# Dilated and plain sliding-window attention with a gated FFN: residue-order attention blocks, v turned on chip, and a list scheduler that sets every engine's order

## Chip, cores and metric

The kernel runs on one core of a Trainium2 chip. The metric is the device time of one execution in microseconds. Before the change it is 392.39 us, the median of three runs (391.03 to 394.54); the profiled execution spans 389.0 us from its first to its last instruction. TensorE (PE in the profile, with PEld for its weight loads), VectorE (DVE), ScalarE (ACT), GpSimd (POOL) and SyncE (SP) each run their own queue in order, and DMA transfers are issued from the queues of POOL (loads) and SP (stores).

## The reference

Shapes: 8 batches, 8 heads, 576 positions, head size 64; the FFN has 512 inputs, 1024 hidden, 512 outputs. Everything comes and goes in float32.

```python
scores = (1/sqrt(64)) * q @ k.T
rel = pos[:, None] - pos[None, :]
mask_plain = (rel >= 0) & (rel < 32)                       # heads 0 to 3
mask_dil   = (rel >= 0) & (rel < 128) & (rel % 4 == 0)     # heads 4 to 7
attn = softmax(where(mask, scores, -1e9))
x = (attn @ v) as [8*576 tokens, 8*64]
out = ((x @ w1) * (x @ w2)) @ w3 @ w_out
```

A query of the first four heads sees at most 32 preceding positions (its own among them); a query of the last four sees every fourth of the 128 preceding ones, which are positions of its own residue modulo 4.

## The kernel before

**The FFN.** `w3 @ w_out` is multiplied once into `wf` (`fuse_t`, L383, turns a slice of w3 on TensorE; `fuse_m`, L392, multiplies). The 4608 tokens go in 9 tiles of 512. For each tile `ffn1` (L341) does, for 8 slices of the hidden size, four matmuls of 512 columns with w1 into one PSUM bank, ACT's copy of them to SBUF (L360), four with w2 into another bank, and VectorE's product of the two (L361). `ffn2` (L363) multiplies the gated tile with `wf`, 8 matmuls for each 128 tokens; ACT copies the result and SP stores it. All three use the PSUM tag `f`, with three banks.

**Attention.** A batch has four steps (class `Step`, L191): head group u = 0 (plain) or 1 (dilated), in two halves each. `transposes` (L180) turns q and k of one group with VectorE, so that partitions hold 32 of the 64 head dimensions of four heads; a position then takes two bf16 values, 4 bytes. It is called from within `scores` when a group begins, that is, it enters VectorE's queue just before the matmuls that need it. `scores(hp)` (L196) does two of the four heads: plain heads in blocks of 96 queries and 128 keys, at contiguous positions; dilated heads in blocks of 72 queries of one residue, read with a step of four positions from the same tile:

```python
lhsT=kt[prt, k0 : k0 + st * (P - 1) + 1 : st, c],
rhs=qt[prt, q0 : q0 + st * (nq - 1) + 1 : st, c],      # st is 1 or 4
```

ACT takes the exponential (L225), VectorE multiplies by a 0/1 mask (L230). `values` (L245) multiplies by v, which has a column of ones, so that the sums come along (L258 plain, L274 dilated); `norm` (L234) divides on VectorE; `xpose` (L283) turns the result on TensorE (L290, L302) and copies it into `XT`, the FFN's input, in token order: plain heads by VectorE (L296), dilated ones by ACT, with a step of four tokens (L309).

**v.** It is loaded twice over in ready form: `vp` (L102) with 32 rows of overlap between blocks for plain heads, and `vd` (L120), eight DMAs a batch, for dilated heads.

**Order.** Each engine's order is the order of the program. Loads are issued at the start (L408 to L421): q, k and v of batch 0, then w1 and w2, then q, k, v of batch 1, w_out and w3. Batch 0's attention is written in full before any FFN work. Afterwards `point()` (L434), called inside the FFN's loops, puts in pieces of the later batches' attention by a table of marks (`np.interp` over `xs`, `ys`); when a batch's pieces are done, the loads of the next but one are issued on POOL. PSUM: scores two banks, values two, transposes one, FFN three.

Of the kernel before, what the change touches and what calls it, by code (L numbers as in the profile page):

```python
# [10 lines left out]
P = 128  # L11
# [8 lines left out]
S = 576  # L20
D = 64
ROWS = 18
HALF = 288
PADK = 32
PITCH = 80
ETW = 4 * HALF + 64
TB = 512


@with_exitstack  # L30
def kernel(
# [22 lines left out]
    ctx.enter_context(tc.manual_schedule())  # L54

    const = ctx.enter_context(tc.tile_pool(name="const", bufs=1))
    qk_pool = ctx.enter_context(tc.tile_pool(name="qk", bufs=2))
    tr_pool = ctx.enter_context(tc.tile_pool(name="tr", bufs=2))
# [3 lines left out]
    ps_o = ctx.enter_context(tc.tile_pool(name="pso", bufs=1, space=bass.MemoryType.PSUM))  # L62
    ps_x = ctx.enter_context(tc.tile_pool(name="psx", bufs=1, space=bass.MemoryType.PSUM))
    ps_f = ctx.enter_context(tc.tile_pool(name="psf", bufs=3, space=bass.MemoryType.PSUM))
# [7 lines left out]
    mask_pl = const.tile([P, 2, 3, 96], BF16, name="mask_pl")  # L72
    mask_di = const.tile([P, 2, 2, 72], BF16, name="mask_di")
    NV = 2
    vps = [const.tile([P, 24, PITCH], BF16, name=f"vp{i}") for i in range(NV)]
    vds = [const.tile([P, 4, 2, 4, PITCH], BF16, name=f"vd{i}") for i in range(NV)]
    NET = 3
    ets = [const.tile([P, ETW], BF16, name=f"et{i}") for i in range(NET)]
    NKT = 2
    kts = [const.tile([P, PADK + S, 2], BF16, name=f"kt{i}") for i in range(NKT)]  # L80
    qts = [const.tile([P, S, 2], BF16, name=f"qt{i}") for i in range(NKT)]
# [4 lines left out]
    def load_qk(b, us=(0, 1), both=True):  # L86
        for nm, src in (("qn", q), ("kn", k)):
            if (nm, b) not in qk:
                qk[(nm, b)] = qk_pool.tile([P, 2, ROWS * D], BF16, tag=nm, name=nm)
            t = qk[(nm, b)]  # L90
            flat = src[b].rearrange("(u h) s d -> u (h s d)", u=2)
            if both:
                nc.gpsimd.dma_start(
                    out=t, in_=flat.rearrange("u (p x) -> p u x", p=P)
                )
            else:
                for u in us:
                    nc.gpsimd.dma_start(
                        out=t[:, u, :], in_=flat[u].rearrange("(p x) -> p x", p=P)
                    )  # L100

    def load_vp(b):  # L102
        vp = vps[b % NV]
        base = v[b, 0, 0, 0:1]
        off = base.offset

        def src(p0, n, j0, nj):
            return bass.AP(
                tensor=base.tensor,
                offset=off + (96 * j0 - 32 + p0) * D,  # L110
                ap=[[D, n], [96 * D, nj], [1, D]],
            )

        if b == 0:
            nc.gpsimd.dma_start(out=vp[32:P, 0:1, 0:D], in_=src(32, 96, 0, 1))
            nc.gpsimd.dma_start(out=vp[:, 1:24, 0:D], in_=src(0, P, 1, 23))
        else:
            nc.gpsimd.dma_start(out=vp[:, :, 0:D], in_=src(0, P, 0, 24))

    def load_vd(b):  # L120
        vd = vds[b % NV]
        for h in range(4):
            for w in range(2):
                nc.gpsimd.dma_start(  # L124
                    out=vd[:, h, w, :, 0:D],
                    in_=v[b, 4 + h, 64 * w : 64 * w + 512, :].rearrange(
                        "(p r) d -> p r d", r=4
                    ),
                )

    def load_w12(c):
        for dst, src in ((w1_sb, moe_w1), (w2_sb, moe_w2)):
            nc.gpsimd.dma_start(
                out=dst[:, :, 256 * c : 256 * (c + 1)],
                in_=src[:, 256 * c : 256 * (c + 1)].rearrange("(a p) f -> p a f", p=P),
            )

    def load_wo():
        nc.gpsimd.dma_start(out=wo_sb, in_=moe_w_out.rearrange("(a p) f -> p a f", p=P))

    w3t = {}

    def load_w3(ft):
        w3t[ft] = w3_pool.tile([P, d_ff], BF16, tag="w3", name="w3n")
        nc.gpsimd.dma_start(out=w3t[ft], in_=moe_w3[ft * P : (ft + 1) * P, :])


    def build_constants():
        make_identity(nc, ident)
        for t in ets:  # L150
            nc.gpsimd.memset(t[:, 4 * HALF : ETW], 0.0)
        for t in kts:
            nc.gpsimd.memset(t[:, 0:PADK, :], 0.0)
        for t in vps:
            nc.gpsimd.memset(t[:, :, D : D + 1], 1.0)
        for t in vds:
            nc.gpsimd.memset(t[:, :, :, :, D : D + 1], 1.0)
        nc.gpsimd.memset(vps[0][0:32, 0:1, 0:D], 0.0)
        nc.gpsimd.memset(mask_pl, 1.0)
        nc.gpsimd.affine_select(  # L160
            out=mask_pl, in_=mask_pl, compare_op=AL.is_ge, fill=0.0,
            base=32, pattern=[[0, 2], [0, 3], [1, 96]], channel_multiplier=-1,
        )
        nc.gpsimd.affine_select(
            out=mask_pl, in_=mask_pl, compare_op=AL.is_ge, fill=0.0,
            base=-1, pattern=[[0, 2], [0, 3], [-1, 96]], channel_multiplier=1,
        )
        nc.gpsimd.memset(mask_pl[0:32, 0, 0, :], 0.0)
        nc.gpsimd.memset(mask_di, 1.0)
        nc.gpsimd.affine_select(  # L170
            out=mask_di, in_=mask_di, compare_op=AL.is_ge, fill=0.0,
            base=0, pattern=[[0, 2], [56, 2], [1, 72]], channel_multiplier=-1,
        )
        nc.gpsimd.affine_select(
            out=mask_di, in_=mask_di, compare_op=AL.is_ge, fill=0.0,
            base=31, pattern=[[0, 2], [-56, 2], [-1, 72]], channel_multiplier=1,
        )


    def transposes(b, u):  # L180
        for nm, dst, pad in (("qn", qts[u], 0), ("kn", kts[u], PADK)):
            t = qk[(nm, b)]
            nc.vector.transpose(  # L183
                out=dst[:, pad : pad + S, :]
                .rearrange("p s c -> p (s c)")
                .bitcast(U32)
                .rearrange("p (j a) -> p a j", a=ROWS),
                in_=t[:, u, :].bitcast(U32).rearrange("p (a i) -> p a i", a=ROWS),
            )

    class Step:  # L191
        def __init__(self, n, b, u, hf):
            self.n, self.b, self.u, self.hf = n, b, u, hf
            self.et = ets[n % NET]

        def scores(self, hp):  # L196
            u, hf = self.u, self.hf
            if hf == 0 and hp == 0:
                transposes(self.b, u)
            qt, kt = qts[u], kts[u]  # L200
            sp = ps_s.tile([P, 2, TB], F32, tag="s", name="sp")
            if u == 0:
                blocks = [
                    (96 * (3 * hf + m), 96 * (3 * hf + m), 96, 96 * m, 1) for m in range(3)
                ]
            else:
                blocks = []
                for bl in range(4):
                    r, w = 2 * hf + bl // 2, bl % 2
                    blocks.append((PADK + 64 * w + r, 288 * w + r, 72, 72 * bl, 4))  # L210
            for k0, q0, nq, c0, st in blocks:
                for c in range(2):
                    for g in range(2):
                        prt = slice(32 * (2 * hp + g), 32 * (2 * hp + g) + 32)
                        nc.tensor.matmul(  # L215
                            out=sp[:, g, c0 : c0 + nq],
                            lhsT=kt[prt, k0 : k0 + st * (P - 1) + 1 : st, c],
                            rhs=qt[prt, q0 : q0 + st * (nq - 1) + 1 : st, c],
                            start=(c == 0),
                            stop=(c == 1),  # L220
                        )
            ev = self.et[:, 2 * hp * HALF : 2 * (hp + 1) * HALF].rearrange(
                "p (g x) -> p g x", g=2
            )
            nc.scalar.activation(out=ev, in_=sp[:, :, 0:HALF], func=ACT.Exp, scale=scale)  # L225
            if u == 0:
                mk = mask_pl[:, hf, :, :].rearrange("p m x -> p (m x)")
            else:
                mk = mask_di.rearrange("p r w x -> p (r w x)")
            nc.vector.tensor_tensor(  # L230
                out=ev, in0=ev, in1=mk.unsqueeze(1).to_broadcast([P, 2, HALF]), op=AL.mult
            )

        def norm(self, o, nq, nj, xo):  # L234
            rcp = wk_pool.tile([P, 2, 6], F32, tag="rcp", name="rcp")
            ov = o[0:nq, :, 0 : nj * (D + 1)].rearrange("p h (j e) -> p h j e", e=D + 1)
# [126 lines left out]
    def ffn2(t, tb, point):  # L363
        point()
        y = ps_f.tile([P, d_model], F32, tag="f", name="y")
        for f in range(KFF):
            if f == KFF // 2:
                point()
# [131 lines left out]
```

The softmax here doesn't subtract the row's maximum and nothing guards it: scores larger than these inputs give would overflow.

## Time and profile before

| | before |
|---|---|
| time, median of 3 | 392.39 us |
| span of the profiled execution | 389.0 us |
| mean granted TensorE clock | 0.918 |
| matmuls of `ab` (ffn1), `y` (ffn2), `wf` in the trace | 548, 275, 61; mean 406, 403, 422 ns |
| scores: dilated, plain | 512 matmuls, mean 314 ns; 384, mean 234 ns |
| POOL: issues of `vd` | 64, 743 ns each |
| HBM read, written | 44.03 MB, 9.44 MB |

How to read it: a row of a group gives the line, the engine, the operands with partitions x elements, the count, then busy time and the mean of one, then how long the engine had been idle before such instructions and what ended that. A matmul's duration contains its way through the array; several are in flight, so the distance between starts, not the duration, is what one costs. The trace lacks a few matmul records (548 of 576 `ab`). The 40 digits of a slice row are tenths of busy time in slices of 9.7 us. In a timeline, "x12" merges twelve instructions that follow each other, and the number after the start is the time from the first's start to the last's end. The PEclk row has no record ahead of 46 us and shows 9 there.

### The profile page before, as it was taken

How to read it: one execution, taken by the hardware profiler on the slowest of the kernel's cores; microseconds unless marked ns; L12 is line 12 of the kernel's file. 1: busy time of each engine (PE TensorE's matmuls, PEld its weight loads, DVE VectorE, ACT ScalarE, POOL GpSimd, SP SyncE). 2: the span in 40 equal slices, each digit the busy share in tenths (PEclk: the TensorE clock that was granted, in tenths of full speed). 3: DMA queues.
4: the chain of work that ended last, by engine and by line, in shares of the span. 5: the costliest groups of instructions: out<-in, count | busy, mean ns of one | idle time of the engine just before them, and what ended most of it. 6: DMA issues, size and time to landing. Idle time of an engine off the chain costs nothing. (4 is left out here: it accounts for less than half of the span.)

```text
span 389.0 us, 6039 instructions
## 1 busy us (share of the span) xinstructions
PE 314.3 (81%) x2516; PEld 166.6 (43%) x2560; DVE 171.7 (44%) x288; ACT 135.9 (35%) x213; POOL 87.4 (22%) x131
## 2 busy tenths in 40 slices
PE   0382768887887989987987979697969798899995
PEld 0261335343553545443543445254534354444442
DVE  2553456455344453566335644455354644222220
ACT  1222314441443433434342523252325234433332
POOL 8884544632000521015200620060000000000000
PEclk9999989796997998999896989798988899999998
DMA  3999999996600579009920977072000000111103
GB/s 62 150 167 199 152 207 198 157 119 124 41 2 0 35 128 185 33 29 82 176 41 27 83 122 96 27 70 40 28 2 27 29 27 31 51 56 54 53 32 136
DMA packets 74492, 31.86 MB, mean 82 GB/s; under 512 B 59616, under 2 KB 64736, under 8 KB 74464
## 3 DMA queue, kind: packets, MB, share of 16 engines
q0 software_dynamic: 69280, 22.02, 52.5%
q1 hardware_dynamic: 5184, 9.44, 6.5%
q8 instruction: 20, 0.33, 0.3%
q14 instruction: 8, 0.07, 0.0%
HBM read 44.03 MB, written 9.44 MB: 137 GB/s over the span
## 5 line engine op out<-in xcount | busy, mean ns | idle before, releaser
L350 PE MATMUL ab<-XT,w_sb 128*128 128x512 bf16 x548 | 151.2, 406 | 9.1 <-ACT XT L309 6.4
L215 PE MATMUL sp<-qt,kt 32*128 32x72 bf16 (+1 forms) x896 | 58.3, 279 | 46.9 <-DVE kt L183 44.0
L350 PEld LDWEIGHTS <-w_sb 128*128 128x128 bf16 x576 | 53.2, 103 | 63.0 <-issue 17.8
L225 ACT ACTIVATE et<-sp 128x576 bf16<-128x576 f32 x64 | 41.8, 653 | 100.9 <-PE sp L215 100.9
L124 POOL DMA_DIRECT2D vd<-in_v_dram x64 | 47.2, 743 | 130.3 <-PE o L274 109.2
L215 PEld LDWEIGHTS <-kt 32*128 32x128 bf16 x896 | 43.5, 128 | 74.4 <-DVE kt L183 43.6
L369 PE MATMUL y<-wf_sb,gt 128*128 128x512 bf16 x275 | 74.2, 403 | 1.1 <-issue 0.8
L361 DVE TENSOR_TENSOR gt<-ab,asb 128x512 bf16<-128x512 f32 x72 | 49.6, 689 | 57.6 <-PE ab L350 56.6
L360 ACT CAST asb<-ab 128x512 bf16<-128x512 f32 x72 | 42.1, 585 | 72.7 <-PE ab L350 61.5
L369 PEld LDWEIGHTS <-gt 128*128 128x128 bf16 x288 | 26.7, 101 | 36.0 <-issue 10.5
L230 DVE TENSOR_TENSOR et<-et,mask_di 128x576 bf16<-128x576 bf16 x32 | 14.7, 458 | 57.5 <-ACT et L225 57.5
L377 ACT COPY osb<-y 128x512 f32<-128x512 f32 x36 | 21.1, 585 | 50.1 <-PE y L369 47.0
L238 DVE TENSOR_TENSOR xo<-o,rcp 72x512 bf16<-72x512 f32 (+1 forms) x48 | 37.2, 775 | 1.7
L230 DVE TENSOR_TENSOR et<-et,mask_pl 128x576 bf16<-128x576 bf16 x32 | 14.7, 458 | 40.4 <-ACT et L225 39.9
L309 ACT COPY XT<-x 128x288 bf16<-128x288 bf16 x32 | 23.1, 852 | 14.5 <-PE x L302 14.5
L183 DVE STREAM_TRANSPOSE qt<-qn 128x576 uint32<-128x576 uint32 x16 | 20.0, 1249 | 8.2 <-DMA qn<-in_q_dram 8.2
L237 DVE RECIPROCAL rcp<-o 72x8 f32<-72x8 f32 (+1 forms) x48 | 10.1, 210 | 27.3 <-PE o L258 14.3
L183 DVE STREAM_TRANSPOSE kt<-kn 128x576 uint32<-128x576 uint32 x16 | 19.8, 1239 | 1.9 <-DMA kn<-in_k_dram 1.9
L398 PE MATMUL wf<-wo_sb,w3T 128*128 128x512 bf16 x61 | 17.5, 422 | 0.4 <-issue 0.3
L274 PEld LDWEIGHTS <-et 128*128 128x128 bf16 x256 | 13.6, 108 | 9.6 <-issue 2.4
L274 PE MATMUL o<-vd,et 128*128 128x65 bf16 x256 | 15.1, 208 | 1.3 <-DVE xo L238 1.2
L302 PE MATMUL x<-ident,xo 72*128 72x72 bf16 x128 | 9.7, 206 | 7.0 <-DVE xo L238 5.7
(40 smaller groups left out, 122.8 us busy)
## 6 DMA issues: line engine op xcount, KB each, us to landing
out_dram<-osb SPq DMA_DIRECT2D x36, 256.0 KB, 2.0
vd<-in_v_dram POOLq DMA_DIRECT2D x64, 64.0 KB, 3.9
qn<-in_q_dram POOLq DMA_DIRECT2D x7, 576.0 KB, 6.3
kn<-in_k_dram POOLq DMA_DIRECT2D x7, 576.0 KB, 9.2
vp<-in_v_dram POOLq DMA_DIRECT2D x7, 384.0 KB, 7.9
w_sb<-in_moe_w_dram POOLq DMA_DIRECT2D x8, 256.0 KB, 7.2
w3n<-in_moe_w_dram POOLq DMA_DIRECT2D x8, 256.0 KB, 11.5
wo_sb<-in_moe_w_out_dram POOLq DMA_DIRECT2D x1, 1024.0 KB, 9.2
```

The lines of the kernel that those rows point to most:

```text
L124: nc.gpsimd.dma_start(out=vd[:, h, w, :, 0:D], in_=v[b, 4 + h, 64 * w : 64 * w + 512, :].rearrange("(p r) d -> p r d", r=4),)
L183: nc.vector.transpose(out=dst[:, pad : pad + S, :] .rearrange("p s c -> p (s c)") .bitcast(U32) .rearrange("p (j a) -> p a j", a=ROWS), in ...
L215: nc.tensor.matmul(out=sp[:, g, c0 : c0 + nq], lhsT=kt[prt, k0 : k0 + st * (P - 1) + 1 : st, c], rhs=qt[prt, q0 : q0 + st * (nq - 1) + 1 : ...
L225: nc.scalar.activation(out=ev, in_=sp[:, :, 0:HALF], func=ACT.Exp, scale=scale)
L230: nc.vector.tensor_tensor(out=ev, in0=ev, in1=mk.unsqueeze(1).to_broadcast([P, 2, HALF]), op=AL.mult)
L238: nc.vector.tensor_tensor(out=xo[0:nq, :, 0:nj, :], in0=ov[:, :, :, 0:D], in1=rcp[0:nq, :, 0:nj].unsqueeze(3).to_broadcast([nq, 2, nj, D]) ...
L274: nc.tensor.matmul(out=o[:, hp, j * (D + 1) : (j + 1) * (D + 1)], lhsT=self.et[:, c0 : c0 + P], rhs=vd[:, h, w, 2 * self.hf + r, 0 : D + 1 ...
L309: nc.scalar.copy(out=dst[:, 2 * self.hf + r, :, :], in_=xv[:, r, :, :])
L350: nc.tensor.matmul(out=ps, lhsT=w_sb[:, c, f * P : (f + 1) * P], rhs=XT[:, c, t0 : t0 + TB], start=(c == 0), stop=(c == DCH - 1),)
L360: nc.scalar.copy(out=a_sb, in_=ps)
L361: nc.vector.tensor_tensor(out=gts[t][:, f, :], in0=pss[1], in1=a_sb, op=AL.mult)
L369: nc.tensor.matmul(out=y, lhsT=gts[t][:, f, tb * P : (tb + 1) * P], rhs=wf_sb[:, f, :], start=(f == 0), stop=(f == KFF - 1),)
```

## The change

The kernel is rewritten around the same FFN. It does this:

- **Residue order.** q is turned so that positions lie by residue modulo 4 (144 positions each), and for dilated heads k too. Both groups then use blocks of 96 queries against 128 keys at contiguous places, and one step does all four heads, on four row groups of the array, into four PSUM banks. Where a block of 96 crosses from one residue to the next, the mask cuts it. `XT` holds tokens in residue order, and the stores put each row back at its place in the output, four rows apart.
- **Bias in batches 0 and 1.** There, a matmul with the identity puts a large negative bias into PSUM ahead of the scores, and the multiplication by the mask falls away. Later batches multiply by the mask, as before.
- **v turned on chip in batches 0 and 1.** v is loaded like q and k in long rows, turned by VectorE, then on TensorE (`v_back`), and copied to its place by ACT or VectorE (`v_keep`). Later batches load v without overlap (one DMA for plain heads, eight for dilated ones), and VectorE copies the 32 rows of overlap (`halo_v`).
- **Weights** come in halves; constants other than the masks move from POOL to VectorE; 24 matmuls on a tile of zeros run at the start.
- **PSUM**: scores four banks in one buffer; four banks, as places that the scheduler gives out, for FFN, values and transposes.
- **A list scheduler.** Every piece of work is a `Task` with an engine, an assumed duration, the tasks that it needs, and a priority. `Plan.run` simulates the five engines with these numbers and gives an order; the instructions are then written out in it. Attention has priority on TensorE, and the scores of later batches are held back until the FFN has come so far (`paced`, LEAD). Loads come in a fixed order: q and k of batch 0, its v, w1 and w2, w_out, w3, then batch 1.

Its purpose is to shorten the work of attention, to let the FFN begin before batch 1 is loaded, and to keep TensorE from waiting. The diff, cut to its core:

```diff
+class Plan:
+    def run(self):
...
+                for e in engines:
+                    if free[e] > now:
+                        continue
...
+                    for r, t in waiting[e]:
+                        if r > now or (t.slot and not open_):
+                            continue
+                        if best is None or t.prio < best[1].prio:
+                            best = (r, t)
...
+    ets = [const.tile([P, 4 * VC + 32], BF16, name=f"et{i}") for i in range(4)]
+    kts = [const.tile([P, 2, PADK + S, 2], BF16, name=f"kt{i}") for i in range(2)]
+    qts = [const.tile([P, 2, S, 2], BF16, name=f"qt{i}") for i in range(2)]
...
+    def halo_v(b):
+        vp = vps[b % 2]
+        nc.vector.tensor_copy(out=vp[0:32, :, 1:6, 0:D], in_=vp[96:128, :, 0:5, 0:D])
...
+    def v_back(b, u, half):
+        x = bank([P, 3, 2, P], BF16, "vx")
+        for mm in range(3):
+            n0 = QB * (3 * half + mm)
+            for c in range(2):
+                nc.tensor.transpose(
+                    out=x[:, mm, c, :], in_=vts[0][:, u, n0 : n0 + P, c], identity=ident
...
+            self.sp = ps_s.tile([P, 4, TB], F32, tag="s", name="sp")
+            if biased:
+                for g in range(4):
+                    nc.tensor.matmul(
+                        out=self.sp[:, g, 0:VC],
+                        lhsT=ident,
+                        rhs=bias[:, self.kind(), :, :],
+                        start=True,
+                        stop=False,
+                    )
+            for mm in range(3):
+                m = 3 * hf + mm
+                for c in range(2):
+                    for g in range(4):
+                        prt = slice(32 * g, 32 * g + 32)
...
+                        nc.tensor.matmul(
+                            out=self.sp[:, g, QB * mm : QB * mm + QB],
+                            lhsT=kt[prt, u, QB * m : QB * m + P, c],
+                            rhs=qq,
...
+            row = b * S + 4 * (x % RUN) + x // RUN
+            nc.sync.dma_start(
+                out=out[row : row + 4 * (n - 1) + 1 : 4, :], in_=o_sb[at - c0 : at - c0 + n, :]
+            )
...
+    for u in range(2):
+        loads_rows("qn", 0, (u,))
+        loads_rows("kn", 0, (u,))
+    loads_rows("vn", 0)
...
+    lw12 = [loads_w12(0), loads_w12(1)]
...
+                s = add("S" + n, "PE", 480, T[u], st.scores, b - 99, after=[prev["s"]])
+                e = add("E" + n, "ACT", 1150, [s], st.exps, 10 * b + 1, lat=100, after=[prev["e"][i]])
+                m = add("M" + n, "DVE", 680, [e, mk], st.masks, 10 * b + 2, lat=80)
...
+        a = add(f"A{t}.{f}", "PE", 864, need + wl + free, lambda: up(t, f, w1_sb, "a"), seq, slot=True)
...
+    for b, i, t in paced:
+        pair = int(9 * (b - LEAD) + 2.25 * i)
+        if pair > 0:
+            t.after.append(pairs[pair])
+            t.deps.append(pairs[pair])
+
+    order, _ = plan.run()
+    for t in order:
+        plan.now = t
+        t.fn()
```

## The prediction

> **What bounds the kernel now.** I read the page's busy table and 40 slices first, then TensorE's waits between 46 and 332 us, then the timeline around the longest of them.
>
> ```profile
> span 389.0 us, 6039 instructions
> PE 314.3 (81%) x2516; PEld 166.6 (43%) x2560; DVE 171.7 (44%) x288; ACT 135.9 (35%) x213; POOL 87.4 (22%) x131
> PE   0382768887887989987987979697969798899995
> PEclk9999989796997998999896989798988899999998
> ```
>
> TensorE is the bound, but 81% flatters it, since a busy matmul need not be at its peak. The true floor: FFN matmuls of 512 columns follow each other every 216 ns in the chain of waits at the end (16 of `ab` in 3.45 us). There are 576 of `ab`, 288 of `y` and 64 of `wf`: 928 x 0.216 = 200 us. The rest of 389 us is attention, idle time and a slow clock. TensorE's waits from 46 to 332 us:
>
> ```profile
> PE sp L215 <- DVE kt L183: 26.4, 12, 3.1
> PE ab L350 <- ACT XT L309: 5.5, 7, 0.9
> PE x L302 <- DVE xo L238: 3.8, 6, 1.3
> ```
>
> One wait dominates: scores wait for the two transposes that `scores` itself puts at the end of VectorE's queue at each change of head group. All other waits of TensorE in this stretch add to 15 us. One of the twelve, in the timeline:
>
> ```profile
> 204.07 0.69 DVE L361 TENSOR_TENSOR gt<-ab,asb 128x512 bf16<-128x512 f32 x1 [2.30 <-PE ab L350]
> 204.68 1.25 DVE L183 STREAM_TRANSPOSE qt<-qn 128x576 uint32<-128x576 uint32 x1
> 205.76 1.24 DVE L183 STREAM_TRANSPOSE kt<-kn 128x576 uint32<-128x576 uint32 x1
> ...
> 207.06 0.66 PE L215 MATMUL sp<-qt,kt 32*128 32x96 bf16 x12 [2.17 <-DVE kt L183]
> ```
>
> These 12 matmuls take 0.66 us; a group of the same form takes 0.43 at 166.71 (below). The stall has also cost the clock. The clock record after 46 us holds twelve stretches at half speed, 3.4 or 6.8 us each, 61 us in all; windows of 2 us show an empty or half-empty PE just ahead of nearly all of them. Half of 61 is 31 us of lost work. The 9s of the first PEclk slices deceive: at 42 us `ab` matmuls still come every 0.43 us, so everything before 46 us ran cold.
>
> Last, what attention costs a warm TensorE:
>
> ```profile
> 158.53 1.28 PE L215 MATMUL sp<-qt,kt 32*128 32x72 bf16 x16
> ...
> 159.74 0.60 PE L369 MATMUL y<-wf_sb,gt 128*128 128x512 bf16 x2
> ```
> ```profile
> 166.70 0.29 PEld L215 LDWEIGHTS <-kt 32*128 32x128 bf16 x12 [2.46 <-DVE kt L183]
> 166.71 0.43 PE L215 MATMUL sp<-qt,kt 32*128 32x96 bf16 x12 [0.92 <-DVE kt L183]
> 167.07 0.55 PEld L350 LDWEIGHTS <-w_sb 128*128 128x128 bf16 x4
> 167.07 1.04 PE L350 MATMUL ab<-XT,w_sb 128*128 128x512 bf16 x4
> ```
>
> Read from the start of a group to the start of the next: dilated scores hold PE 1.21 us for 16 (76 ns each), plain ones 0.36 for 12 (30 ns). Value matmuls take 31 ns each (8 in 0.25 at 168.81), transposes of 96 columns some 42. A batch is thus 4 x 1.21 + 4 x 0.36 scores, 56 x 0.031 values and about 1 of transposes: 9 us, 72 for eight. Check from 46 to 332 us: FFN and w3 151, attention 62, slow clock 31, idle 41: 285 of 286.
>
> **What the skill says.** SBUF — State Buffer, "Door 1: The DMA port swizzle", has SBUF read in 16-byte lines, with a penalty where each access goes to a new one. Dilated q and k are read at every fourth position of 4 bytes: 16 bytes, a line each; 76 ns against 30 agrees. TensorE: Matmul & The Clock Gate, "Part 1: The HAM clock gate", says that an idle window (about 3.4 us) halves PE's clock and a busy one restores it; the stretches of 3.4 and 6.8 us agree, though gaps of 2 to 3 us already set them off here. The same page, "Back-to-back issue gap", gives N/2.4 + 2.5 ns per warm matmul: 216 at 512, as measured. VectorE: DVE Perf Modes, "The perf-mode tier table", gives an SBUF bf16 copy of 2048 elements as 693 ns; no row here shows one.
>
> **The change, part by part.**
>
> *Residue order and 96-query blocks.* Both head groups now have 96 queries per block, on four row groups at once, from contiguous 4-byte steps: 24 matmuls per step, four steps per batch. The strided 76 ns goes. Per step: at 30 ns each 0.72 us; if the four row groups leave only the weight loads, 0.29/12 x 24 = 0.58. I take 0.65; with values 12 x 0.031 = 0.37 and six transposes 0.25, a step is 1.27 and a batch 5.1, against 9. That saves 3.9 us a batch, 27 for batches 1 to 7, all on the bounding engine. The kept copies get cheaper too: the stride-4 XT copies of ACT (852 ns for 288) become runs of 24 or more, at 160 + 0.83 ns an element by ACT's rows of 512 (585) and 1024 (1012): 0.40.
>
> *Bias instead of mask, v turned on chip, both in batches 0 and 1.* Batch 1 gets 16 bias matmuls of 288 columns, 122 ns each by the formula: 2.0 us; and 24 transposes of v at 56 ns: 1.3. It loses four mask multiplies on VectorE. Batch 0's lie in the head.
>
> *VectorE's order.* Transposes are now put ahead by the scheduler, with two buffers of whole batches. I cost the wait at nothing where a batch's loads are early: VectorE has the room to hide them. Its load per batch of 9 FFN pairs, with slopes from rows (f32 from PSUM 155 + 1.04 ns an element; bf16 158 + 0.52): gates 9 x 0.69 = 6.2, masks 4 x 0.76 = 3.0, reciprocals 8 x 0.2 = 1.6, norms of 384 elements 8 x 0.55 = 4.4, kept copies 4 x 0.31 = 1.2, transposes about 5.2 (the split ones pay a fixed cost twice), halo copy of 2560 elements 0.8 by the skill's price, 2.7 at one element a cycle. Sum 22.5 to 24.3. TensorE needs, per batch, 9 x 1.73 + 4.5 x 1.73 + 5.1 = 28.4. VectorE is 79 to 86% busy: not the bound, but tight. ACT: 9 + 4.5 copies x 0.585, four exps of 1152 elements at 1.13, four copies: 14 of 28.
>
> *PSUM.* Scores take four banks in one buffer; FFN, values and transposes share four. Behind an A matmul group waiting for a bank stands everything on PE. A bank is held 1.7 us by a group of `ab` (0.86 fill, 0.69 evacuation), so two groups in flight leave two banks for attention. I keep the 15 us of other waits in 286 us, 5%, as the rate of such stalls: 0.05 x 243 = 12 us.
>
> *The head.* Before, the first `ab` starts at 42 us. Batch 1's q and k are issued behind ten v loads, w1 and w2, and PE's queue puts their scores first: it sits idle 6.3 us until 39.6. Now tile 0's FFN follows batch 0 alone. POOL makes five q, k, v issues and the masks (eleven instructions of 0.2 to 1 us) by 10.5 us. Then four steps, each held by its exp: warm 0.65 + 0.5 bias + 0.15 + 1.13 = 2.4, cold (12 scores took 0.60 at 11.3 us) 3.6; then values, norms, transposes and copies of the last step, 3.2. Batch 0 ends between 23 and 28 us; I take 26. w1 and w2 are there: 3.9 MB at some 190 GB/s (the fourth and seventh of the DMA slices show 199 and 198), from 3.3 us, is 24 us. Until batch 1 is there (8.8 MB, 50 us, plus 10 to 12 for its chain) PE has tile 0 (13.8), w3's fusing (17.4), `y` of tile 0 (6.9) and batch 1's own 8.4: 46 us of work, so the gap is filled. The 24 warm-up matmuls lie beside loading. I add 2 us for a first cold window at 26 us.
>
> *Stores.* Rows four apart, about 67 DMAs of 2 KB rows instead of 36. SP's queue does nothing else and the queue's share is 6.5%: nothing.
>
> *Loads.* v drops from 14.7 to 9.4 MB read; batches 2 to 7 issue nine v DMAs each on POOL, as now, and POOL is 22% busy: nothing.
>
> **Sum.** TensorE work from 26 us: 200.4 + 64 x 0.056 for w3 + 6 x 5.1 + 8.4 = 243. Span 26 + 2 + 243 + 12 + 4 (last matmul to the end, as now) = 287; the time exceeds the span by 3.4 us now. Forecast 290 us.
> From above: 392 - 16 (head) - 26 (transpose wait) - 31 (clock) - 27 (scores) + 3 (bias, v) = 295, before any gain on the other idle waits. The two ways agree; I take 290.
>
> **Rivals.**
> A, the clock keeps halving: VectorE, four fifths busy and strictly in order, delays evacuations, PE pauses 2 us here and there, and half the clock stretches stay. For: gaps of 2 us were enough before. Against: the transposes, the one long wait, move ahead. If the clock is at half for 21% of the stretch as now (61 of 286), PE loses 0.11 x 243 = 27 us: 317.
> B, the head gains nothing: batch 0 takes until 42 us as the first `ab` does now, as DMA or the longer mask building holds it. For: POOL and DMA are busy nearly the whole head. Against: fewer bytes come first. 290 + 16 = 306.
> C, even better: no stalls, scores at 0.58: 290 - 12 - 2 = 276.
> D, slower than before: the fixed orders don't fit the chip, each engine waits in its own order for another's, and the clock, once half, stays there as it did until 46 us. Attention's stretch holds about 190 us of PE work; at half speed for 60% of it, +114: 404. Against: slots and in-order waits existed before, with only 15 us of them.
>
> **How the numbers follow.** Forecast (280 to 302) 0.60; A 0.18; B 0.10; C 0.07; D 0.05. The likeliest is 290. Range: down to 272 (no stalls, 23 us head, scores 0.58), up to 322 (A, with the halo copy at its slow price). What is left out is D and the far ends of A and C. Faster by over 1%: all but D, and a little of A gone further: 0.94; same 0.01; slower 0.05.
>
> **What would show it.** Right: no wait of scores for `kt` beyond 2 us after 60 us; at most two or three half-clock stretches past 70 us; dilated and plain scores both under 0.75 us for 24; first `ab` at 24 to 30 us; VectorE near 65% busy and PE over 90% from 60 us on. Wrong: `ab` or `y` waiting for banks freed by VectorE for over 20 us in sum, half clock in the middle, or PE idle between 45 and 70 us for batch 1.

## The result, and the profile after

The changed kernel takes 277.59 us (median of four runs, 276.21 to 278.35) against 391.71 us before in the same series; the ratio is 0.709, with a 95% interval of 0.704 to 0.714. The forecast was 290 us. The kernel before takes 382 to 394 us from one execution to the next, and its profiled one is among the slower, so savings on it are counted below from its faster executions, with medians of 382.6, 383.1 and 382.9 us in the three later series. Counted so, the changed kernel saves 105 us and not 114. The changed kernel itself ran in the first series only, so differences of 1 to 2 us from it say little.

The page of the changed kernel, in the lines that answer to those shown of before:

```profile
span 274.5 us, 5945 instructions
PE 258.3 (94%) x2440; PEld 132.8 (48%) x2440; DVE 168.6 (61%) x342; ACT 124.7 (45%) x207; POOL 65.7 (24%) x105
PE   8577997899889989999999999999999999999993
DVE  3674435999999989999799555566654232242220
PEclk9989999999999999999999999999999999999999
```

TensorE's row is 9 almost throughout, and its clock row is now honest: the clock record begins at 5.6 us, with one stretch at half speed at 12.5 us (3.4 us) and none until the kernel is over. The 7 at 41 us and the 8 behind it are a hole that run 11 is about. VectorE shows mostly 9 from the eighth to the twenty-second slice (48 to 151 us), more than I had reckoned.

TensorE's waits from 24 us to the end, longest first:

```profile
PE x L412 <- DVE xo L401: 1.3, 3, 0.7
PE wf L506 <- ACT w3T L501: 1.2, 1, 1.2
PE x L494 <- DVE wf_sb L516: 1.1, 2, 0.8
PE sp L344 <- DVE qt L289: 0.8, 1, 0.8
PE ab L442 <- ACT asb L453: 0.7, 1, 0.7
```

Scores wait for turned q or k once, 0.8 us; all waits of this view add to 5.7 us. The timeline shows why, and what a step of attention costs:

```profile
147.24 0.44 PE L344 MATMUL sp<-qt,kt 32*128 32x96 bf16 x24
147.35 0.31 DVE L431 COPY XT<-x 128x288 bf16<-128x288 bf16 x1
147.61 1.04 PE L442 MATMUL ab<-XT,w_sb 128*128 128x512 bf16 x4
147.69 0.40 ACT L429 COPY XT<-x 128x288 bf16<-128x288 bf16 x1
147.73 1.41 DVE L289 STREAM_TRANSPOSE kt<-kn 128x320 uint32<-128x320 uint32 x2
```

The transposes run while TensorE is in the FFN and nothing waits for them. The 24 score matmuls of a step take 0.37 us from their start to the start of the next group. The kept copies take 0.31 and 0.40 us, as worked out.

Where the time went, from the first `ab` matmul to the last matmul. I took the distance from the start of each group to the start of the next in the timelines, and set idle time apart (the rows are good to about 1 us):

| us | before | after |
|---|---|---|
| first `ab` at | 42.0 | 24.9 |
| FFN (`ab`, `y`, `wf`) | 223.9 | 202.9 |
| scores, with bias | 46.4 | 12.8 |
| values | 15.6 | 11.7 |
| transposes, with w3's | 14.3 | 13.6 |
| idle | 43 | 5 |
| last matmul at | 384.8 | 270.3 |

The FFN did not get less work: its 21 us are, but for a slow start before 46 us, its share of the half-clock stretches, which are gone. Of 114.5 us between the spans of the two profiled executions, the first `ab` gives 17, the idle time 38, the scores 34 (with their share of the clock), the clock in the FFN 21, the rest 4.

### The profile page after: what moved, and what is told of

Same layout as the page of the kernel before. It is cut to its first block, busy times and chain, and to the rows that moved or that the text cites. A ratio compares the mean times of both kernels' runs of the same rounds, so it can differ in the third digit from the quotient of the medians.

```text
span 274.5 us, 5945 instructions
## 1 busy us (share of the span) xinstructions
PE 258.3 (94%) x2440; PEld 132.8 (48%) x2440; DVE 168.6 (61%) x342; ACT 124.7 (45%) x207; POOL 65.7 (24%) x105
## 4 chain that ended last, share of the span: by engine, by line
PE 84%; DVE 7%; DMA 3%; issue 2%; ACT 1%; POOL 1%; DVEq 0%; ACTq 0%; POOLq 0%
PE ab L442 44%; PE y L464 22%; PE wf L506 5%; DMA vn<-in_v_dram 3%; PE sp L344 3%; PE vo L377 3%; DVE xo L401 3%; PE x L412 2%; PE vx L298 1%; PE x L494 1%; DVE rcp L395 1%; PE sp L327 1%; DVE et L360 1%; DVE gt L457 1%; DVE wf_sb L516 1%
## 5 line engine op out<-in xcount | busy, mean ns | idle before, releaser
L442 PE MATMUL ab<-XT,w_sb 128*128 128x512 bf16 x576 | 135.7, 380 | 1.1 <-ACT asb L453 0.7
L354 ACT ACTIVATE et<-sp 128x1152 bf16<-128x1152 f32 x32 | 36.6, 1143 | 16.0 <-PE sp L344 15.9
L210 POOL DMA_DIRECT2D vp<-in_v_dram x48 | 30.5, 644 | 32.0 <-PE vo L377 9.9
L401 DVE TENSOR_TENSOR xo<-vo,rcp 96x384 bf16<-96x384 f32 x64 | 35.2, 551 | 1.9
L289 DVE STREAM_TRANSPOSE qt<-qn 128x320 uint32<-128x320 uint32 (+1 forms) x32 | 21.6, 681 | 4.3 <-DMA qn<-in_q_dram 4.0
L377 PE MATMUL vo<-vp,et 128*128 128x65 bf16 x384 | 17.7, 194 | 1.3 <-DVE vp L311 0.8
L360 DVE TENSOR_TENSOR et<-et,mask 128x1152 bf16<-128x1152 bf16 x24 | 17.8, 745 | 0.0
L412 PE MATMUL x<-ident,xo 96*128 96x96 bf16 x192 | 14.2, 207 | 2.2 <-DVE xo L401 2.1
L344 PE MATMUL sp<-qt,kt 32*128 32x96 bf16 x768 | 14.3, 204 | 0.8 <-DVE qt L289 0.8
L344 PEld LDWEIGHTS <-kt 32*128 32x128 bf16 x768 | 9.7, 94 | 8.5 <-issue 6.4
```

What stands on the lines that cost most here:

```text
L210: nc.gpsimd.dma_start(out=vp[32 + p0 : 32 + p0 + n, 4:8, m, 0:D], in_=v_rows(b, 4, 4 * t0 + res, [[4 * D, n], [S * D, 4], [1, D]]),)
L289: nc.vector.transpose(out=o, in_=i)
L344: nc.tensor.matmul(out=self.sp[:, g, QB * mm : QB * mm + QB], lhsT=kt[prt, u, QB * m : QB * m + P, c], rhs=qq, start=(c == 0 and not biase ...
L354: nc.scalar.activation(out=ev, in_=self.sp[:, :, 0:VC], func=ACT.Exp, scale=scale)
L377: nc.tensor.matmul(out=self.o[g // 2][:, g % 2, mm, :], lhsT=self.et[:, c0 : c0 + P], rhs=vp[:, 4 * self.u + g, 3 * self.hf + mm, 0 : D + ...
L401: nc.vector.tensor_tensor(out=self.xo[0:QB, :, gs, :].rearrange("p m g d -> p g m d"), in0=self.o[pg][0:QB, :, :, 0:D], in1=self.rcp[0:QB, ...
```

## Experiments

My theory: three things make up the gain, namely the transposes' place in VectorE's queue together with the clock that its stalls halved, the strided reads of dilated scores, and the head. The rivals: the clock halves for another reason, the strides are hidden, the head's gain is load order alone. No run takes the new PSUM layout, the double buffers of turned q and k, the halved weight loads or the scattered stores by themselves.

**1. Transposes half a group earlier, in the kernel before.**

```diff
-            if hf == 0 and hp == 0:
+            if hf == 0 and hp == 0 and not self.turned:
                 transposes(self.b, u)
...
-                a.append(lambda st=st: st.scores(0))
+                nxt = steps[st.n - steps[0].n + 1 :][:1] if st.hf == 1 else []
+                for x in nxt:
+                    x.turned = True
+                a.append(lambda st=st, nxt=nxt: (st.scores(0), [transposes(x.b, x.u) for x in nxt]))
```

> The kernel before, with one edit: the two transposes of the next head group enter VectorE's queue half a group earlier (after the first scores of the group's second step), so that scores no longer meet them. Theory of the prediction: the waits of scores for kt after 46 us (26 us) go, and with them nearly all of the half-clock stretches (31 us): about 335 us, between 328 and 345, with at most three half-clock stretches after 60 us. Rival 1, the clock halves for another reason: only the 26 us go, about 365 us with ten or more stretches. Rival 2, the transposes block VectorE's other work in the new place and PE waits for that instead: 380 to 392 us.

Measured: 353.71 us (352.21 to 354.19), 29 us less than 382.6. TensorE's waits from 46 to 300 us, the timeline of VectorE at 64 us, and the clock row (slices of 8.8 us):

```profile
PE o L275 <- DVE xo L239: 8.0, 2, 7.8
PE ab L354 <- ACT XT L310: 6.4, 8, 0.9
PE x L303 <- DVE xo L239: 3.3, 6, 0.9
```
```profile
64.69 1.26 DVE L183 STREAM_TRANSPOSE qt<-qn 128x576 uint32<-128x576 uint32 x1 [5.46 <-DMA qn<-in_q_dram]
67.48 1.26 DVE L183 STREAM_TRANSPOSE kt<-kn 128x576 uint32<-128x576 uint32 x1 [1.53 <-DMA kn<-in_k_dram]
```
```profile
PEclk9999999759999999999999999999999999999999
```

The wait for kt has left the list, 26 us in the kernel before. Between the two profiled executions, idle time falls by 18 us and the FFN by 15 with the same work. Half-clock stretches fall from twelve (61 us) to one, of 13.7 us, and that one begins at 66 us, inside the single long stall that is left: moved forward, batch 2's transposes now stand in VectorE's queue ahead of batch 2's load, and everything behind them waits 7.8 us. So here the clock followed the stalls, and rival 1 falls. The number was missed by 19 us, of which the new stall (7.8) and its half-clock stretch (half of 13.7, 7 us of lost work) make up 15. Putting work earlier in an in-order queue is safe only as far as its own data is early; the scheduler of the changed kernel knows when a load should land.

**2. Dilated scores at neighbouring positions, in the kernel before.**

```diff
-                    blocks.append((PADK + 64 * w + r, 288 * w + r, 72, 72 * bl, 4))
+                    blocks.append((PADK + 64 * w + r, 288 * w + r, 72, 72 * bl, 1))
```

> The kernel before, with dilated scores reading q and k at neighbouring positions instead of every fourth (same number of matmuls, same sizes; the dilated heads then get scores of the wrong positions, so this part of the computation is changed). Theory: a group of 16 falls from 1.21 to 16 x 0.030 = 0.48 us; 28 groups after batch 0: -20 us, about 371 us. Rival: dilated scores are held by something else (72 columns, the exp, the order), and the group stays near 1.2 us: 389 to 393 us.

Measured: 361.29 us (357.90 to 364.49); 357.90 and 359.10 us stand against 382.53 and 382.75 of the kernel before, 24 us less. A dilated group of 16 and what follows it, and the clock row (slices of 8.9 us):

```profile
141.10 0.45 PE L215 MATMUL sp<-qt,kt 32*128 32x72 bf16 x16
141.48 0.82 PE L350 MATMUL ab<-XT,w_sb 128*128 128x512 bf16 x2
```
```profile
PEclk9999998789899899999999999999969899999999
```

0.38 us in place of 1.21. In the sum over TensorE's groups, scores fall from 46.4 to 22.6 us, while the waits for kt stay (28.8 us). The strided reads thus cost some 24 us themselves. Half-clock time is 27 us here against 61 in the profiled execution of the kernel before; for its execution of 382.53 us, with a mean clock of 0.948 over 380.8 us, it comes to 2 x 0.052 x 380.8 = 40 us, an estimate from these two figures. So the clock stayed up more often with the same stalls around; the last section shows where that comes from.

**3. The changed kernel with dilated reads at every fourth position again.**

```diff
-                            qq = qt[prt, u, QB * m : QB * m + QB, c]
+                            qq = qt[prt, u, 32 * m : 32 * m + 4 * (QB - 1) + 1 : 4, c]
+                        kk = kt[prt, u, QB * m : QB * m + P, c]
+                        if u == 1:
+                            kk = kt[prt, u, 16 * m : 16 * m + 4 * (P - 1) + 1 : 4, c]
...
-                            lhsT=kt[prt, u, QB * m : QB * m + P, c],
+                            lhsT=kk,
```

> The changed kernel, with the dilated scores (24 matmuls a step) reading q and k at every fourth position again (from places that exist, so the dilated heads get scores of wrong positions). Theory, the price is per matmul as before: 24 x 0.076 = 1.82 us in place of 0.37, in 14 steps after batch 0: +20 us, about 298 us. Rival, four row groups in turn hide the slow reads as they hide the rest: 24 x 0.038 = 0.9 us, +7 us, about 285 us.

Measured: 292.41 us (290.01 to 292.79), 14.8 us more, between the two figures.

```profile
159.05 1.26 PE L347 MATMUL sp<-qt,kt 32*128 32x96 bf16 x24
160.25 1.04 PE L445 MATMUL ab<-XT,w_sb 128*128 128x512 bf16 x3
```

1.20 us for 24, 50 ns each: more than contiguous (15 ns), less than 76. Over 14 steps the extra 0.83 us is 11.6 us; the rest lies in the head, where the first `ab` comes 4.0 us later (28.9 us). The head is at half clock for 17 us here, but that alone isn't it: run 6 has as much and takes no longer. The expectation had left out that a block has 96 columns here and 72 in the kernel before. A dilated step took 2 x 1.21 us there and 1.20 here, a plain one 2 x 0.37 there and 0.37 here: four row groups in place of two halve the strided price just as they halve the other. So the two gains multiply: with four row groups in place the layout is worth 0.83 us a step, with two it was worth 1.66.

**4 and 10. How many row groups lie side by side.** The first edit changed the order within a block of 96 queries only:

```diff
-                for c in range(2):
-                    for g in range(4):
+                for c, g in [(c, 2 * gp + x) for gp in range(2) for c in range(2) for x in range(2)]:
                         prt = slice(32 * g, 32 * g + 32)
```

> The changed kernel, with the 24 score matmuls of a step in another order: first those of row groups 0 and 1 in turn, then those of 2 and 3, as the kernel before did. Theory: a matmul of 96 columns costs 40 ns divided by the row groups that run side by side; with two in turn a step takes 24 x 0.030 = 0.72 us in place of 0.37, in 28 steps after batch 0: +10 us, about 288 us. Rival: weight loads or issue set the pace of these matmuls, and the order is worth nothing: 277 to 279 us.

Measured: 277.74 us (276.43 to 278.82), no change; a step still takes 0.38 us. The edit was too weak: after the first two matmuls of groups 0 and 1, those of 2 and 3 can lie beside their second ones. So the pairs went outermost:

```diff
-            for mm in range(3):
-                m = 3 * hf + mm
-                for c in range(2):
-                    for g in range(4):
+            for gp, mm in [(gp, mm) for gp in range(2) for mm in range(3)]:
+                m = 3 * hf + mm
+                for c in range(2):
+                    for g in (2 * gp, 2 * gp + 1):
```

> The changed kernel, with all 12 score matmuls of row groups 0 and 1 first and then the 12 of 2 and 3 (the earlier run in two groups changed only the order within a block, where two and two could still lie side by side). Theory: row groups in flight together set the price; two at a time give six pairs of 40 ns for each half, 0.48 + 0.13 us a step in place of 0.37: +0.24 in 28 steps, +7 us, 283 to 286 us. Rival: weight loads set the pace (24 in 0.30 us), the step stays at 0.37 and the time at 277 to 279 us.

Measured: 280.29 us (279.05 to 282.77), 2.7 us more.

```profile
157.44 0.54 PE L344 MATMUL sp<-qt,kt 32*128 32x96 bf16 x24
157.92 2.76 PE L442 MATMUL ab<-XT,w_sb 128*128 128x512 bf16 x11
```

0.48 us a step, 0.11 more, and 28 x 0.11 = 3.1 us: less than expected, but the order does count, so weight loads alone don't set the pace. In this step the starts come in pairs, 43 ns apart at first and at the end but about 21 ns apart in the middle, which suggests that the two halves overlap in part; the expected 0.61 us had left that out.

This corrects my reading of the kernel before. I divided 0.36 us by 12 and took 30 ns for a matmul's price. In the trace, the 24 matmuls of a step after start in six rounds of four, at 0, 56, 99, 142, 185 and 228 ns; the 12 of a plain group before start in six rounds of two, at 0, 56, 99, 144, 190 and 234 ns. A round takes some 43 ns with two row groups or with four, and from the last round some 0.13 us pass until the next full-array matmul starts, paid once per group. So twenty-four matmuls on four row groups cost what twelve on two did. The Trainium skill has this in TensorE: Matmul & The Clock Gate, "Part 3: Packing small matmuls", where four row groups give 3.07 times the speed at 512 columns; here, from two row groups to four, 0.37 us hold twice the matmuls of 0.36.

**5. No warm-up matmuls.**

```diff
-    add("warm", "PE", 7000, [c0], warm_up, 0)
```

> The changed kernel without the 24 warm-up matmuls. Theory of the prediction: they lie beside loading and batch 0's chain is held by exp, copies and VectorE more than by PE, but the clock then starts cold at the first FFN matmuls (some 3.4 to 7 us at half speed) and batch 0's matmuls run cold: +2 to +5 us, 280 to 283 us. Rival: batch 0's own matmuls warm the clock as well, nothing changes, 277 to 278.5 us.

Measured: 279.05 us (277.85 to 279.41), 1.5 us more, though the two sets of runs overlap. The clock record begins at 18.9 us in place of 5.6, and the first `ab` starts at 26.6. The theory is half right: batch 0's first matmuls do run cold (four bias matmuls take 1.12 us in place of 0.65) and the head's chain is 1.7 us longer, but the clock is up before the FFN begins, so there is no cold start of the FFN to save.

**6. No bias matmuls.**

```diff
-BIASED = 2
+BIASED = 0
```

> The changed kernel with the mask multiplication in batches 0 and 1 too, no bias matmuls. Theory: PE loses 2.0 us of bias matmuls in batch 1, VectorE gets eight multiplies of 0.75 us; batch 0's chain gets up to 3 us longer but can start 2 us earlier, as scores no longer wait for the masks at 10.5 us: within 2 us of 277.6. Rival: VectorE, over 90% busy from 50 to 100 us, hands the extra 3 us on to PE and batch 0 ends 3 us later: 281 to 284 us.

Measured: 277.25 us (276.63 to 278.08): no difference that the runs show. As far as these runs show, the bias's matmuls and the multiplies that they replace weigh the same. The head is at half clock for 17 us here, and the first `ab` comes at 26.1 us, 1.1 later.

**7. v of batches 0 and 1 loaded in its final form.**

```diff
-    loads_rows("vn", 0)
+    loads_v(0)
...
-        fast = b < 2
+        fast = False
```

> The changed kernel with v of batches 0 and 1 loaded in rows of 64 values by nine DMAs each, as the later batches do, and none turned on chip. Theory: turning v is there to shorten the loads: nine small-row DMAs ahead of w1 and w2 cost some 6 us more of transfer than one long-row DMA, so batch 0 and the first FFN matmuls come 4 to 7 us later: 282 to 285 us. Rival: transfer is hidden behind POOL's masks and batch 0's chain, and PE gains the 1.3 us of v transposes in batch 1: 275 to 278 us.

Measured: 278.71 us (277.49 to 278.94), 1.1 us more, and the two sets of runs overlap. The first `ab` starts at 26.3 us, not at 29 to 32, though the clock is at half from 11.5 to 28.6 us. Turning v on chip is worth about a microsecond at most: if it shortens the transfer, that is mostly hidden.

**8. Batch 1's loads ahead of w1 and w2.**

```diff
+    for nm in ("qn", "kn", "vn"):
+        loads_rows(nm, 1)
     lw12 = [loads_w12(0), loads_w12(1)]
...
-        if b > 0:
+        if b > 1:
             loads_rows("qn", b)
```

> The changed kernel with the loads of batch 1 (q, k, v) ahead of w1 and w2, the order of the kernel before. Theory: the first FFN matmul comes about 9 us later (5.3 MB at 200 GB/s are 9 us of transfer), near 33 us, but batch 1's 7 us of attention on PE then fill part of that gap: +2 to +5 us, 280 to 283 us. Rival B of the prediction, the load order is the head's whole gain: +9 us or more, 287 us and up. Rival, no effect: 277 to 278.5 us.

Measured: 279.88 us (278.93 to 280.72), 2.3 us more, at the low end of the theory. (The kernel before did not load in this order: there w1 and w2 came ahead of batch 1, and only w_out and w3 behind it. The edit goes further.) Batch 1's steps stand before the first `ab`, which comes at 35.4 us, 10.5 later:

```profile
32.30 0.65 PE L327 MATMUL sp<-bias,ident 128*128 128x288 bf16 x4
32.88 0.44 PE L344 MATMUL sp<-qt,kt 32*128 32x96 bf16 x24
...
35.44 0.81 PE L442 MATMUL ab<-XT,w_sb 128*128 128x512 bf16 x2
```

So load order is not the head's whole gain, and the time of the first FFN matmul is not the measure of a head: 10.5 us later, it costs 2.3. What counts is how much of TensorE's work is done by then, and here the scheduler filled the time with batch 1. (The prediction's rival B said something else, that the head gains nothing; the first `ab` at 24.9 us in place of 42.0 answers it.)

**9. The scheduler with wrong durations.**

```diff
+        dur = dur if eng in ("DMA", "SP") or name == "warm" else 700
         self.name, self.eng, self.dur, self.fn, self.prio = name, eng, dur, fn, prio
```

> The changed kernel, where the scheduler believes that every task of TensorE, VectorE and ScalarE (save the warm-up) takes 700 ns, in place of durations that fit the chip; needs, priorities, places and loads stay. Theory (rival D of the prediction in small): fixed orders must fit the chip, so engines wait for each other in the wrong order, PE's waits grow from 6 to 20 us or more and some half-clock stretches come back: 290 to 310 us. Rival: priorities and needs make the order, durations hardly matter: 276 to 281 us.

Measured: 298.30 us (296.08 to 299.50), 20.7 us more, with the same work and the same priorities. TensorE's waits from 24 us on:

```profile
PE sp L345 <- ACT et L355: 4.3, 4, 1.3
PE x L495 <- DMA w3n<-in_moe_w_dram: 2.4, 1, 2.4
PE vo L378 <- DVE et L361: 2.2, 3, 1.1
PE ab L443 <- ACT asb L454: 1.8, 3, 0.7
```

Many small waits of many kinds, 18 us in sum against 5.7, and five half-clock stretches (24 us) where there was none after 16 us. The durations are worth 21 us; the order is not made by needs and priorities alone. Still it is 85 us faster than the kernel before (382.9 us).

**11. A faster version.** (w_out and two slices of w3 ahead of w1 and w2, `BIASED = 0`, and 370 in place of 480 for the scores in the scheduler; the diff shows the loads only)

```diff
-    lw12 = [loads_w12(0), loads_w12(1)]
-    for c in range(2):
-        lwo[c] = load(f"LWO{c}", 600, 3300, [], lambda c=c: load_wo(c))
-    for ft in range(KFF):
-        lw3[ft] = load(f"LW3.{ft}", 550, 1400, [], lambda ft=ft: load_w3(ft))
...
+    ld_wo()
+    ld_w3(0, 2)
+    lw12 = [loads_w12(0)]
+    lw12.append(loads_w12(1))
+    ld_w3(2, KFF)
```

> A version meant to be faster: the changed kernel with w_out and the first two slices of w3 loaded ahead of w1 and w2 (so that fusing w3 fills PE's gaps behind batch 0's attention and is spread among the first FFN matmuls), no bias matmuls, and the scheduler's figure for the scores set to the 370 ns that they take. Theory: PE's gap of 3 us between 40 and 50 us goes, 2 us of bias matmuls go and part of the gaps of the first 25 us: 271 to 275 us. Rival: what is put forward only moves the gap to where w1 and w2 are waited for: 277 to 279 us.

Measured: 273.19 us (272.56 to 274.92), 4.4 us less than the changed kernel's median; the two sets of runs don't overlap. The head of it:

```profile
22.00 0.61 PE L494 MATMUL x<-ident,w3n 128*128 128x128 bf16 x8
...
25.01 1.90 PE L506 MATMUL wf<-wo_sb,w3T 128*128 128x512 bf16 x7 [0.66 <-DVE xo L401]
26.74 0.42 PE L412 MATMUL x<-ident,xo 96*128 96x96 bf16 x6
27.00 1.89 PE L506 MATMUL wf<-wo_sb,w3T 128*128 128x512 bf16 x8
28.73 1.46 PE L442 MATMUL ab<-XT,w_sb 128*128 128x512 bf16 x6
```

Fusing w3 now starts at 22 us, between the last pieces of batch 0. The row of the windows view for 40 to 50 us, of the changed kernel and then of this one (the first figures are TensorE's busy us and its matmuls):

```profile
40.00:50.00 10.00, 7.73 (x53) 4.05 (x52) 5.47 (x9) 3.04 (x3) 2.49 (x4) 1.00 1.11 212
```
```profile
40.00:50.00 10.00, 9.56 (x67) 5.35 (x68) 5.28 (x8) 3.90 (x5) 2.88 (x6) 1.00 1.11 211
```

In the changed kernel the fusing stands alone there, as a chain of TensorE, ACT and TensorE again; with part of it done early and the rest spread among `ab`, TensorE is busy for 9.56 of these 10 us in place of 7.73. The three edits were not run apart; run 6 shows no gain from the one on bias by itself.

**12. Batch 1's attention behind five FFN groups, in the kernel before.**

```diff
-    marks = [(0, 0.0), (14, per), (56, 2 * per + 6)]
+    marks = [(0, 0.0), (5, 0.0), (15, per), (56, 2 * per + 6)]
```

> The kernel before, with batch 1's attention put behind the first five FFN matmul groups (marks 0 until point 5, then batch 1 until point 15). Theory of the prediction's head step: PE's 6 us wait for batch 1's keys is filled with FFN work: -4 to -6 us, 386 to 388 us. Rival: FFN groups before 42 us run cold and batch 1's attention then meets tile 1 late, so the time stays at 390 to 393 us.

Measured: 386.21 us (median of 22 runs, 384.42 to 388.25) against 390.92 (27 runs of before, 382.49 to 393.97). The first `ab` comes at 33.4 us, 8.6 earlier, and the medians differ by the expected 4.7 us; but against 382.9 us the ratio is 1.006 (1.002 to 1.010), a little slower. So a gain is not shown. The profiled run has 65 us of half clock, 20.5 of them in one stretch from 54.9 us on, against 61 in the profiled execution of the kernel before and an estimated 40 in its execution of 382.53 us (run 2), which would take back what the earlier start gains.

## Why the prediction was right

The range held and the mechanism is the one forecast; the time lies a little under the forecast's own band of 280 to 302. What it said would show it right came: scores waited for turned q or k once, for 0.8 us; no half clock fell past 70 us; 24 scores took 0.37 us; the first `ab` came at 24.9 us; from 60 us on VectorE was 63% busy and TensorE 97%. By its own sum (26 + 2 + 243 + 12 + 4 = 287 us of span, against 274.5):

- *Head, 26.* Measured 24.9. The chain was right in its parts (masks ready at 10.5 us, as said, and the bias waited for them). That this 17 us is worth 16 in the end was the wrong way to see it: run 8 moved the first `ab` by 10.5 us for 2.3. The head's share of the gain is that TensorE has useful work from 25 us on without a gap; its single terms (load order 2.3, warm-up 1.5, v 1.1, bias 0) are small; that the scheduler makes up for each is likely, but not shown, and no run isolates what the head as a whole is worth.
- *Cold start, 2.* Nothing: the clock is up from 16 us on, and without the warm-up from 18.9 (run 5).
- *TensorE's work, 243.* Measured 240.4 (245.4 from the first `ab` on, less 5 of waits). The scores were mis-sized: 0.65 us a step where 0.37 was measured, and 28 steps give 7.8 us; what failed there is the price of 30 ns a matmul, taken from two row groups and counted for each of 24 matmuls on four. The price goes by rounds: six rounds of 43 ns and a tail of 0.13 us, before and after. The tail alone would not have set it right (24 x 20 ns + 0.13 = 0.61 us). Values (11.7 against 10.4), transposes (13.6 against 11.9) and FFN (202.9 against 200.4) came out a little dearer, by 5.5 us in sum; small groups pay the tail as well (six value matmuls at 65.65 us hold 0.28 us, twelve at 56.66 us 0.37).
- *Other waits, 12.* Measured 5.7: the rate of 5% was too high. It had been taken over from the kernel before, where a hand-made order produced it. Run 9 gives back 12 us of waits by wrong durations alone, so the rate belongs to the order, not to the hardware.
- *Tail, 4.* 4.2.

These terms (-1.1, -2, -2.6, -6.3, +0.2) give 275.2, near the 274.5 measured; the waits of 24 to 24.9 us stand in two of them. The forecast's 3.4 us from span to time set the span of one execution against the median of others; in each execution on record the two are 1.7 to 2.3 us apart, 1.7 in the profiled one here. The terms that were too dear outweigh those that were too cheap, and the scores' error (-7.8) was in good part covered by the rest of TensorE's work (+5.5): that the work came out within 3 us of 243 is partly luck.

*Transposes' wait (26) and clock (31) removed, 57.* Shown by run 1 as far as it goes: 29 us from the one edit (37 between the two profiled spans), with 15 held back by a late load; and by the clock record after. *Scores, 27:* the layout gives 24 by itself in run 2; the four row groups then halve what is left (runs 3 and 10).

*VectorE 79 to 86% busy.* It was 90 to 98% in the windows of 10 us from 50 to 130 us, since the scheduler runs attention ahead of the FFN, and only near 58% from 150 to 210. Rival A rested on this load; its premise was met more than fully, and yet TensorE's waits that VectorE ended add to 1.6 us in those 80 us. The scheduler's priorities put the evacuations first in VectorE's order, and the transposes and masks fill what is left; that this is the reason is likely, but no run took it away. What the halo copy costs (850 ns in the mean) fits the lower price taken, 0.8.

*Rival D* appears in small in run 9, and is far from 404 us. *Rival C* was, by its number (276), what came, but that is luck: it kept 0.58 us for a step, and no wait at all.

## What to carry to other kernels

Look at what stands in an in-order queue just ahead of the work that the bound engine waits for: two transposes of 1.25 us, put in the wrong place, cost 26 us of waits in sum and more through the clock (15 us of FFN in run 1). An order computed from measured durations is worth its upkeep (21 us here between right and flat figures), and with it single decisions in the head were cheap to get wrong (0 to 2.3 us in runs 5 to 8). When a small matmul is priced from a group, count the rounds of row groups that lie side by side, not the matmuls, and take the group's fixed tail out.

## What the runs showed of the hardware that I had not expected

- Matmuls of 32 x 96 follow each other on a row group every 43 ns or so, whether two row groups work side by side or four; a group of 24 on four and one of 12 on two both end in about 0.37 us, with some 0.13 us from the last start to the next full-array matmul.
- A 16-byte step in both operands costs TensorE some 1.9 ns a column: a round of 72 columns on two row groups takes 137 ns (kernel before), one of 96 on four takes 177 (run 3). Without the step it is 36 ns for 72 columns (run 2) and 43 for 96.
- VectorE at over 90% for 80 us held TensorE up for 1.6 us in sum.
- The clock goes by fixed stretches of time. In all 14 traces it changes only at multiples of 3.41 us from its other changes. The traces, divided on that grid from the first clock record to some 6 us before the end, hold 1158 stretches. Of those at full clock, 33 had 2.0 us or more between TensorE's records, and each was followed by half clock; 971 had less than 0.9 us, and none was; of the 75 in between 13 were, so that more than idle time must count there. Of those at half clock, 46 of the 54 with less than 0.5 us of idle time were followed by full clock, and none of the 25 with more.

So the sum of the idle time in one stretch matters, not the length of one wait. In run 9 half clock follows waits of 1.3 us and less that fall together, at 71.8, 191.3 and 225.4 us. In the kernel before, a stretch holds one wait of 0.87 us and 1.24 us of the next, which is 2.17 us long, and half clock follows; in run 2 the same two waits fall into two stretches, with 1.3 and 1.8 us of idle time, and the clock stays up. The rows of the windows view for these stretches, of the kernel before and then of run 2, give the length, TensorE's busy us and its matmuls, and the clock (1.00 or 0.50):

```profile
202.72:206.13 3.41, 1.30 (x6) 1.00 0.00 0
206.13:209.54 3.41, 2.48 (x20) 0.50 0.00 0
```
```profile
186.42:189.84 3.42, 2.12 (x12) 1.00 0.00 0
189.84:193.25 3.41, 1.65 (x24) 1.00 0.00 0
193.25:196.66 3.41, 3.38 (x33) 1.00 0.20 77
```
